# Residual beside the exponentials, sums beside the normalized weights, and a larger part of one output-weight unit kept on chip

## The chip, the core and the metric

The kernel runs on one core of a Trainium2 chip. The metric is the device time of one execution in microseconds. The core has a matrix engine (TensorE, in the profile PE for matmuls and PEld for weight loads), VectorE (DVE), ScalarE (ACT), GpSimd (POOL) and a queue that only issues DMAs (SyncE, SP). ScalarE and GpSimd can issue DMAs too. Each engine works through its own list of instructions in order and waits on semaphores for the others. On-chip memory has 128 partitions; matmul results go to PSUM banks.

## The reference

Two branches share one layer norm of x (2048 rows of 1024) and are added to x.

```python
xn = _layernorm(x, axis=-1)
return x + _A_ref(xn, A_mem0, A_Wq, A_Wk, A_Wv, A_Wo, A_seg_len) + _B_ref(xn, B_w1, B_b1, B_w2, B_b2)
```

Branch B is a dense layer to 3584, an approximate GELU and a dense layer back. Branch A is a recurrence over 64 segments of 32 rows:

```python
h = jnp.concatenate([mem, xs], axis=1)          # 8 memory rows, 32 rows of x
q, k, v = (einsum('btd,dhe->bhte', h, W) for W in (Wq, Wk, Wv))     # 32 heads of 128
p = _softmax(where(mask, einsum(q, k) * scale, -1e9))
o = einsum('bhte,hed->btd', einsum(p, v), Wo)
mem = o[:, :M, :]                               # handed to the next segment
outs.append(o[:, M:, :])
```

So each segment must have the memory rows of the one before, and each needs all four weights, 32 MB in bfloat16[...].

## The kernel before

**Two stages.** The first (up to L639) computes layer norm and branch B for all rows, and leaves in DRAM, for each segment, a row block `hr_d[s]` of 128 partitions by 512 columns. Its columns 0 to 255 are the turned x rows of segment s; columns 256 to 511 of block s + 1 hold the residual, x plus branch B, that is to be added to the output of segment s. The second stage is the loop over 64 segments (L715).

**A main row set and a left one.** A segment's main product takes 24 of its x rows and the 8 memory rows, 32 in all. The other 8 x rows of four segments are gathered to a left set of 32 rows, and pass through the weights once per group of four, spread over its segments. In segments with number 1 modulo 4 and in the last (`left_o`), one output product of 64 rows covers both sets. Such a segment has two residuals: `st["res"]` and, from `hrL_d`, `st["resL"]`.

**Weights.** The weights are cut into 64 units of 128 by 2048 (512 KB). The order of a segment is K, Q, K, Q, V, V in half passes of eight units and O of sixteen. 46 units stay in on-chip memory; 18 are streamed for each segment. Of these two are copied from PSUM banks (`IN_PSUM`, `IN_BANKS`), by VectorE at L246. One more (`PART`, the thirteenth of O counted from zero) is partly resident: its first `PART_COLS` = 768 columns stay in `part_home`, the others are loaded. The stream has six places; when TensorE has used a unit (`unit_done`), SyncE starts the load of the next into its place (`start_stream`), and waits for its turn in order.

**Small homes.** Three tensors at fixed places share a scratch area. `half_home` (1024 columns) is `part_home` in columns 0 to 767 and `pr_all`, the home of the exponentials of the attention scores, in the others. `hr_home` (512 columns) holds the x rows in columns 0 to 255, read by the K, Q and V products as `hT`, and `res_home` in columns 256 to 511. `pd_main` (320 columns) holds the normalized attention weights of the main keys, made by VectorE at L896 from the exponentials; L900 makes those of the left keys (`pd_left`) and is the last to read `pr_all`. The values product (L915) reads `pd_main`.

**Order around the change.** In half pass V, 1, after unit 4, `sums(1)` starts the second normalization: a product with ones on TensorE, a logarithm and two exponentials on ScalarE (L886, L889), then L896 and L900 on VectorE. At the end of that half pass, `load_x_rows(s + 1)` (L268) loads the next segment's block: for s + 1 above 5 all 512 columns in one DMA of 128 KB, x rows and residual together; before that 256 columns, and the residual by a DMA of its own at L1039. ScalarE issues these for segments 0 to 4, GpSimd for the others. The left residual is loaded into `pr_all` after O unit 1 (L1072). The values product of the second half stands after O unit 5 (in segments 3 modulo 4 after units 4 and 6). After O, the output goes to `o_sb` (L1081 or L1084), `put_mem` turns the eight memory rows on TensorE (L291) and writes them beside the x rows in `hr_home` (L295); the next segment's K pass reads both. Then the residual is added in place (L1104), and the sums are stored by GpSimd: four DMAs of 24 rows (L1137), or in `left_o` segments four to `outL_d` (L1109) and from there to the output (L1134).


Of the kernel before, what the change touches and what calls it, by code (L numbers as in the profile page):

```python
# [14 lines left out]
ALU = mybir.AluOpType  # L15
PSUM = bass.MemoryType.PSUM

P = 128
S = 2048
DM = 1024  # L20
# [17 lines left out]
NX = 24  # L38
# [16 lines left out]
WARM = 16  # L55
NPAIR = 9
AT_BANKS, AT_PART = 5, 4
PART_COLS = 768


def pass_order():
# [28 lines left out]
def kernel(  # L90
# [16 lines left out]
    nc = tc.nc  # L107
# [3 lines left out]
    out_flat = out.rearrange("b s d -> (b s) d")  # L111
# [6 lines left out]
    Wo_v = A_Wo.rearrange("h e d -> e h d")  # L118
# [6 lines left out]
    hr_d = dram.tile([NSEG + 1, P, 512], BF16, name="hr_d")  # L125
    hrL_d = dram.tile([NGRP + 1, P, 512], BF16, name="hrL_d")
# [13 lines left out]
    half_home = nc.alloc_sbuf_tensor_at("half_home", [P, DM], BF16, offset=SCRATCH)  # L140
    hr_home = nc.alloc_sbuf_tensor_at("hr_home", [P, 512], BF16, offset=SCRATCH + 2048)
    pd_main = nc.alloc_sbuf_tensor_at("pd_main", [P, 320], BF16, offset=SCRATCH + 3072)

    part_home, pr_all, res_home = half_home[:, 0:PART_COLS], half_home[:, PART_COLS:DM], hr_home[:, 256:512]
    slabs = ctx.enter_context(tc.tile_pool(name="slabs", bufs=1))
    consts = ctx.enter_context(tc.tile_pool(name="consts", bufs=1))
    hrp = ctx.enter_context(tc.tile_pool(name="hrp", bufs=1))
# [11 lines left out]

    qL_last = consts.tile([P, 16, SEG], BF16, name="qL_last")  # L160
    qL = [consts.tile([P, 16, SEG], BF16, name="qL"), qL_last]
    ident = res_home[:, 0:P]
    make_identity(nc, ident)
    ident_mem = consts.tile([P, 4, NL], BF16, name="ident_mem")
    nc.vector.tensor_copy(out=ident_mem[:, :, :], in_=ident.rearrange("p (j t) -> p j t", j=4)[:, :, NX:SEG])
# [2 lines left out]
    for j in range(4):  # L168
# [11 lines left out]
        out=m, in_=m, pattern=[[1, NX]], compare_op=ALU.is_ge, fill=0.0, base=0, channel_multiplier=-1,  # L180
    )
    for half in range(2):
        m = mask_left[0:SEG, :, 8 - 8 * half:16 - 8 * half]
        nc.gpsimd.affine_select(
            out=m, in_=m, pattern=[[-8, GRP], [0, 8]], compare_op=ALU.is_ge, fill=0.0, base=0, channel_multiplier=1,
        )
        nc.gpsimd.affine_select(
            out=m, in_=m, pattern=[[8, GRP], [1 if half else 0, 8]], compare_op=ALU.is_ge, fill=0.0,
# [28 lines left out]
    def fetch(t, unit):  # L217
        w, i, u = unit
        if unit == PART:
            h = 4 * i + 2 * u  # L220
            nc.sync.dma_start(out=t[:, 0:DM - PART_COLS], in_=Wo_v[:, h, PART_COLS:])
            nc.sync.dma_start(out=t[:, DM - PART_COLS:], in_=Wo_v[:, h + 1, :])
        elif w == "O":
            h = 4 * i + 2 * u
            nc.sync.dma_start(out=t.rearrange("p (h d) -> p h d", d=DM), in_=Wo_v[:, h:h + 2, :])
        else:
            nc.sync.dma_start(out=t, in_=W_v[w][:, i, 2048 * u:2048 * u + 2048])
# [36 lines left out]
    nxt, kept_in = {}, {}  # L264

    def load_x_rows(s, eng=nc.sync):
        n = 512 if s > 5 else 256
        eng.dma_start(out=hr_home[:, 0:n], in_=hr_d[s, :, 0:n])  # L268
        nxt["hT"] = hr_home[:, 0:256].rearrange("p (k t) -> p k t", k=KT)

    def load_left_rows(g, eng=nc.sync):
# [30 lines left out]
    with tc.tile_pool(name="ma", bufs=2) as ma, tc.tile_pool(name="mps", bufs=6, space=PSUM) as mps:  # L302
# [31 lines left out]
        for j in range(4):  # L334
            nc.sync.dma_start(
                out=o_sb[32 * j + NX:32 * j + 32, 0:8, :],
                in_=mem0[:, 256 * j:256 * j + 256].rearrange("m (h e) -> m h e", h=8),
# [4 lines left out]
        for i in range(14):  # L342
            t = slab(f"w2_{i}")[:, :].rearrange("p (c d) -> p c d", d=DM)
# [171 lines left out]
        for tg in range(4):  # L515
            last = tg == 3
            if last:
# [3 lines left out]
                h = 4 * IN_BANKS[1] + 2 * IN_BANKS[2]  # L521
# [12 lines left out]
            for fb in range(FC):  # L534
# [3 lines left out]
                else:  # L538
# [4 lines left out]
                    out=xb[:, :], in_=ps[:, :], func=ACT.Identity, bias=b1col[:, fb:fb + 1], scale=1.0  # L543
# [4 lines left out]
                    out=u[:, :], in0=u[:, :], scalar1=0.044715, scalar2=1.0, op0=ALU.mult, op1=ALU.add  # L548
# [96 lines left out]
    with tc.tile_pool(name="late", bufs=1) as late, \  # L645
# [69 lines left out]
        for s in range(NSEG):  # L715
# [15 lines left out]
            st = {}  # L731
# [301 lines left out]
            else:  # L1033
                at[1] = [lambda: values(0, (0, 1))]

            def load_res():
                st["res"] = res_home
                if s < 5:
                    nc.scalar.dma_start(out=res_home, in_=hr_d[s + 1, :, 256:512])  # L1039

            psV1, psV1L = half_pass("V", 1, left_v[1], at)
            st["V", 1] = values_out(psV1, sp.tile([P, 512], BF16, name="v", tag="a"), nc.scalar.copy)
# [1 line left out]
                left_values(1, psV1L)  # L1044
            if not final:
                load_x_rows(s + 1, nc.scalar if s < 5 else nc.gpsimd)
            else:
                nc.gpsimd.dma_start(out=res_home, in_=hr_d[s + 1, :, 256:512])
            if first:
                load_left_rows(g + 1, nc.gpsimd)  # L1050

# [4 lines left out]
                at = {5: [lambda: values(1, (0, 1))]}  # L1056
            if left_v[1] and not first:
                at[9] = [lambda: left_values(1, psV1L)]
            at.setdefault(0, []).append(load_res)
            psX = new_acc()  # L1060
            for n, unit in enumerate(O_UNITS):
                t = unit_tile(unit)
                if n == NPAIR and not left_o:
                    st["folded"] = fold(psX)
                    psX = new_acc()
                o_product(n, t, psX)
                unit_done(unit)
                for fn in at.get(n, ()):
                    fn()
                if n == 1 and left_o:  # L1070
                    st["resL"] = pr_all
                    (nc.scalar if s < 5 else nc.gpsimd).dma_start(  # L1072
                        out=st["resL"][:, :], in_=hrL_d[og, :, 256:512]
                    )
            nw = 2 if left_o else 1
            if not final:
                o_sb = nat_home
# [20 lines left out]
            for w, r in reversed(list(enumerate(tiles))):  # L1098
                if left_o:
                    o = psX[:, 256 * w:256 * w + 256].rearrange("p (h e) -> p h e", e=32)  # L1100
                else:
                    o = o_sb[:, 0:8, :]
                r_rows = r.rearrange("p (h e) -> p h e", e=32)
                nc.vector.tensor_tensor(out=r_rows, in0=o, in1=r_rows, op=ALU.add)  # L1104
                if left_o and not final:

                    for b in range(2):
                        c0 = 256 * (2 * b + w)
                        nc.gpsimd.dma_start(out=outL_d[og, :, c0:c0 + 256], in_=r[64 * b:64 * b + 64, :])  # L1109
# [5 lines left out]
            if final:  # L1115
                engines = [nc.sync, nc.scalar]
                n = 0
                for w, r in enumerate(tiles):
                    for b in range(2):
                        cs = slice(256 * (2 * b + w), 256 * (2 * b + w) + 256)  # L1120
                        pieces = [(rows, slice(64 * b + m0, 64 * b + m0 + NX))]
                        for sl, row in left_rows:
                            p0 = 64 * b + NL * sl
                            pieces.append((slice(row, row + NL), slice(p0, p0 + NL)))
                        for o, i in pieces:
                            engines[n % 2].dma_start(out=out_flat[o, cs], in_=r[i, :])
                            n += 1
            elif left_o:
                pairs = [(out_flat[rows, :], outL_d[og, m0:m0 + NX, :])]
                pairs += [  # L1130
                    (out_flat[row:row + NL, :], outL_d[og, NL * sl:NL * sl + NL, :]) for sl, row in left_rows
                ]
                for o, r in pairs:
                    small.append(lambda o=o, r=r: nc.gpsimd.dma_start(out=o, in_=r))  # L1134
            else:
                for j in range(4):
                    nc.gpsimd.dma_start(out=out_flat[rows, 256 * j:256 * j + 256], in_=res[32 * j:32 * j + NX, :])  # L1137
            if not final:
                hT = nxt["hT"]
        while small:  # L1140
# [34 lines left out]
```

## Time and profile before

| what | value |
|---|---|
| median of 3 runs (lowest, highest) | 1835.91 us (1828.53, 1837.86) |
| the profiled execution | 1839.26 us |
| its span (first to last instruction) | 1837.5 us |
| TensorE matmuls busy | 1717.9 us, 93% |
| VectorE, ScalarE, GpSimd busy | 955.3, 663.8, 284.4 us |
| bytes moved by DMA | 612.94 MB, mean 334 GB/s |
| start of the first segment's products | 417.4 us |
| loads of streamed O units | 256 of 512 KB, 64 of 320 KB |
| loads of x rows by GpSimd (L268) | 58 of 128 KB, 5.5 us to landing (median) |

The page gives each engine's busy time in 40 equal slices, a digit being tenths. A row of the list of waits reads: engine and instruction that stood idle, what ended the wait, the sum in us, how many times, the longest. A row of a timeline reads: start in us, length in us, engine, line, operation, what it writes and reads, and in brackets the idle time of the engine before it with what ended it. A GpSimd row of a DMA is the time to issue it, not to move the data.

### The profile page before, as it was taken

Reading aid. Unit: us, or ns where it says so; the run is one execution under the profiler, and the core shown is the slowest. Engines: PE = TensorE matmul, PEld = TensorE weight load, DVE = VectorE, ACT = ScalarE, POOL = GpSimd, SP = SyncE. Lnnn points to the kernel's source line nnn. Section 1 sums busy time; section 2 is a strip of 40 time slices with the busy share of each in tenths; the row PEclk is TensorE's granted clock in tenths of the full one; section 3 lists DMA queues with packets and bytes.
Section 4 is the critical chain, followed back from the end, with each engine's and each line's share of the span. In section 5 each row is a group of like instructions: output and inputs, shape, how many; then the busy total and the mean of one; then the engine's idle time right before and its main releaser. Section 6 shows DMA issues by size and latency. Waiting matters only on the chain.

```text
span 1837.5 us, 69927 instructions
## 1 busy us (share of the span) xinstructions
PE 1717.9 (93%) x30556; PEld 893.2 (49%) x30576; DVE 955.3 (52%) x2330; ACT 663.8 (36%) x1429; POOL 284.4 (15%) x559
## 2 busy tenths in 40 slices
PE   8999999998999999999999999999999999999997
PEld 4444444444454445454545545454545454545444
DVE  7657483805454545555454555455545454545543
ACT  6334251602333333333333333333333333333333
POOL 0000001501342111111111111112111111111111
PEclk9999999999999999999999999999999999999999
DMA  9931212769999999999999999999999999999998
GB/s 286 313 98 46 55 44 57 260 209 371 397 404 389 391 384 389 381 394 388 373 397 386 400 385 394 374 390 401 389 384 390 383 398 391 397 376 384 389 393 313
DMA packets 229278, 612.94 MB, mean 334 GB/s; under 512 B 46795, under 2 KB 76027, under 8 KB 228972
## 3 DMA queue, kind: packets, MB, share of 16 engines
q1 hardware_dynamic: 207252, 588.05, 84.3%
q0 software_dynamic: 17408, 17.69, 3.0%
q8 instruction: 239, 3.92, 0.8%
q10 hardware_dynamic: 4312, 2.73, 0.5%
q14 instruction: 67, 0.55, 0.1%
HBM read 594.40 MB, written 29.23 MB: 339 GB/s over the span
## 4 chain that ended last, share of the span: by engine, by line
PE 32%; DMA 18%; DVE 4%; ACT 2%; issue 1%; POOL 0%; DVEq 0%; ACTq 0%; SPq 0%
PE acc L739 22%; DMA u<-Wc_K 10%; PE acc L962 6%; DMA outL_d<-half_home 3%; DMA u<-Wc_O 3%; ACT mixed L889 1%; DVE b_oL L804 1%; PE acc L915 1%; DMA hr_home<-hr_d 1%; DVE pd_main L896 1%; PE mixed L848 1%; DMA u<-Wc_V 1%; ACT mixed L886 1%; DMA u<-Wc_Q 0%; PE mixed L854 0%
## 5 line engine op out<-in xcount | busy, mean ns | idle before, releaser
L739 PE MATMUL acc<-u,hr_home 128*32 128x512 bf16 x11520 | 770.8, 380 | 34.0 <-DMA u<-Wc_K 18.2
L739 PEld LDWEIGHTS <-hr_home 128*32 128x32 bf16 x12288 | 342.1, 96 | 317.3 <-issue 57.3
L739 PE MATMUL acc<-u,hrL 128*32 128x512 bf16 x2880 | 248.8, 379 | 3.0 <-DVE folded L978 3.0
L468 PE MATMUL ps<-u 128*128 128x512 bf16 (+1 forms) x920 | 195.7, 375 | 2.0 <-ACT u L388 2.0
L246 DVE TENSOR_SCALAR u<-kept 128x512 uint32<-128x512 uint32 x254 | 163.5, 685 | 35.4 <-PE acc L962 12.3
L962 PE MATMUL acc<-u,d_oL 128*32 128x512 bf16 (+1 forms) x1792 | 153.3, 381 | 11.7 <-DMA u<-Wc_O 9.4
L790 ACT CAST kT<-acc 128x512 bf16<-128x512 f32 x64 | 37.4, 585 | 307.6 <-PE acc L739 307.5
L589 PE MATMUL ps<-u 128*128 128x512 bf16 x657 | 146.2, 379 | 0.8
L962 PEld LDWEIGHTS <-b_oL 128*32 128x32 bf16 (+1 forms) x3381 | 108.4, 98 | 74.5 <-issue 35.9
L896 DVE TENSOR_TENSOR pd_main<-half_home,mixed 128x320 bf16<-128x320 bf16 x128 | 62.4, 487 | 153.2 <-ACT mixed L889 153.2
L468 PEld LDWEIGHTS <-u 128*128 128x128 bf16 x920 | 90.5, 99 | 105.5 <-issue 2.4
L1137 POOL DMA_DIRECT2D out_dram<-hr_home x188 | 96.3, 512 | 294.1 <-DVE hr_home L1104 280.5
L962 PE MATMUL acc<-u,b_oL 128*32 128x256 bf16 (+2 forms) x2062 | 117.1, 289 | 20.2 <-DMA u<-Wc_O 19.5
L804 DVE STREAM_TRANSPOSE b_oL<-b_oL 128x512 bf16<-128x512 bf16 x128 | 90.6, 708 | 64.8 <-ACT b_oL L790 64.8
L268 POOL DMA_DIRECT2D hr_home<-hr_d x58 | 32.8, 565 | 581.3 <-PE acc L739 576.1
L962 PEld LDWEIGHTS <-d_oL 128*32 128x32 bf16 (+1 forms) x2048 | 70.3, 99 | 84.7 <-issue 28.0
L739 PEld LDWEIGHTS <-hrL 128*32 128x32 bf16 x3072 | 82.9, 96 | 51.2 <-issue 7.7
L790 ACT CAST b_oL<-acc 128x512 bf16<-128x512 f32 x128 | 75.1, 587 | 86.1 <-PE acc L739 86.1
L589 PEld LDWEIGHTS <-u 128*128 128x128 bf16 x672 | 65.3, 98 | 77.3 <-DVE g_u L550 0.4
L889 ACT ACTIVATE mixed<-mixed,small_consts 128x160 f32<-128x160 f32 x256 | 94.2, 368 | 8.4
L542 ACT ACTIVATE g_xb<-ps,b1col 128x512 bf16<-128x512 f32 x112 | 76.8, 686 | 55.5 <-PE ps L468 54.7
L794 ACT CAST v<-acc 128x512 bf16<-128x512 f32 x128 | 75.1, 587 | 48.9 <-PE acc L739 48.6
(129 smaller groups left out, 2011.6 us busy)
## 6 DMA issues: line engine op xcount, KB each, us to landing
u<-Wc_K SPq DMA_DIRECT2D x320, 512.0 KB
u<-Wc_V SPq DMA_DIRECT2D x256, 512.0 KB
u<-Wc_O SPq DMA_DIRECT2D x256, 512.0 KB
u<-Wc_Q SPq DMA_DIRECT2D x128, 512.0 KB
u<-Wc_O SPq DMA_DIRECT2D x64, 320.0 KB
u<-in_B_w_dram SPq DMA_DIRECT2D x28, 512.0 KB
hr_home<-hr_d POOLq DMA_DIRECT2D x58, 128.0 KB, 5.5
u<-in_A_Wq_dram SPq DMA_DIRECT2D x14, 512.0 KB
```

What stands on the lines that cost most here:

```text
L246: nc.vector.tensor_single_scalar(out=out, in_=in_, scalar=0, op=ALU.bitwise_or)
L468: nc.tensor.matmul(ps[:, SEG * s0:SEG * s1].rearrange("p (s t) -> p s t", t=SEG), lhsT=w1_sb[fb // 2][:, kt, (fb % 2) * P:(fb % 2 + 1) * P ...
L542: nc.scalar.activation(out=xb[:, :], in_=ps[:, :], func=ACT.Identity, bias=b1col[:, fb:fb + 1], scale=1.0)
L589: nc.tensor.matmul(ps[:, :], lhsT=gts[fc // 4][:, fc % 4, t * P:(t + 1) * P], rhs=w2_sb[fc // 2][:, fc % 2, cs], start=(fc == 0), stop=(fc ...
L739: nc.tensor.matmul(o, lhsT=lhs[:, i, :], rhs=m, start=(i == seq[0]), stop=(i == seq[-1]), tile_position=(0, 32 * j),)
L790: cp(out=out, in_=ps.rearrange("p (h e) -> p h e", e=32))
L794: cp(out=t[:, :], in_=ps[:, :])
L804: nc.vector.transpose(out=home, in_=home)
L889: nc.scalar.activation(out=mixed[:, 160 * b:160 * b + 160], in_=mixed[:, 0:160], func=ACT.Exp, scale=-1.0, bias=off[:, b:b + 1],)
L896: nc.vector.tensor_tensor(out=pdA.rearrange("p c b q -> p b c q"), in0=prA[:, None, :, :].to_broadcast([P, 2, 4, 40]), in1=dd, op=ALU.mult,)
L962: nc.tensor.matmul(acc[r0:r0 + rows, c:c + wide], lhsT=lhs[:, 4 * (i % 4) + 2 * u + k, :], rhs=cols, start=start, stop=stop, tile_position ...
L1137: nc.gpsimd.dma_start(out=out_flat[rows, 256 * j:256 * j + 256], in_=res[32 * j:32 * j + NX, :])
```

## The change

`PART_COLS` goes from 768 to 1024, so `part_home` fills `half_home`, and the streamed rest of the unit is 1024 columns (256 KB). `pr_all` moves to the place in `hr_home` where `res_home` was, and the residual, which lived there, is loaded into `pr_all` once the exponentials are used up; with two residuals the left one goes there and the main one to `pd_main`. The sum of output and residual is written to `pd_main` in segments with one residual, and in place in those with two; the stores read from there.

`load_x_rows` now loads only the x rows. The residual has a DMA of its own in all segments, on the same engine as before: from segment 5 on it is issued after unit 6 of half pass V, 1, ahead of the x rows' load (in `left_o` segments the left residual there, and the main one after O unit 6); in segments 0 to 4 after O unit 0.

```diff
-PART_COLS = 768
+PART_COLS = 1024
...
-    part_home, pr_all, res_home = half_home[:, 0:PART_COLS], half_home[:, PART_COLS:DM], hr_home[:, 256:512]
+    part_home, pr_all = half_home[:, 0:PART_COLS], hr_home[:, 256:512]
...
-            nc.sync.dma_start(out=t[:, 0:DM - PART_COLS], in_=Wo_v[:, h, PART_COLS:])
-            nc.sync.dma_start(out=t[:, DM - PART_COLS:], in_=Wo_v[:, h + 1, :])
+            nc.sync.dma_start(out=t, in_=Wo_v[:, h + 1, :])
...
     def load_x_rows(s, eng=nc.sync):
-        n = 512 if s > 5 else 256
-        eng.dma_start(out=hr_home[:, 0:n], in_=hr_d[s, :, 0:n])
+        eng.dma_start(out=hr_home[:, 0:256], in_=hr_d[s, :, 0:256])
...
+            eng_res = nc.scalar if s < 5 else nc.gpsimd
+
             def load_res():
-                st["res"] = res_home
-                if s < 5:
-                    nc.scalar.dma_start(out=res_home, in_=hr_d[s + 1, :, 256:512])
+                st["res"] = pd_main[:, 0:256] if left_o else pr_all
+                eng_res.dma_start(out=st["res"], in_=hr_d[s + 1, :, 256:512])
+
+            def load_resL():
+                st["resL"] = pr_all
+                eng_res.dma_start(out=st["resL"], in_=hrL_d[og, :, 256:512])
+
+            if s >= 5:
+                at.setdefault(6, []).append(load_resL if left_o else load_res)
 
             psV1, psV1L = half_pass("V", 1, left_v[1], at)
...
                 load_x_rows(s + 1, nc.scalar if s < 5 else nc.gpsimd)
-            else:
-                nc.gpsimd.dma_start(out=res_home, in_=hr_d[s + 1, :, 256:512])
...
-            at.setdefault(0, []).append(load_res)
+            if left_o:
+                at.setdefault(6, []).append(load_res)
+            if s < 5:
+                at.setdefault(0, []).append(load_resL if left_o else load_res)
...
-                if n == 1 and left_o:
-                    st["resL"] = pr_all
-                    (nc.scalar if s < 5 else nc.gpsimd).dma_start(
-                        out=st["resL"][:, :], in_=hrL_d[og, :, 256:512]
-                    )
...
-                nc.vector.tensor_tensor(out=r_rows, in0=o, in1=r_rows, op=ALU.add)
+                sums_home = r if left_o else pd_main[:, 0:256]
+                nc.vector.tensor_tensor(
+                    out=sums_home.rearrange("p (h e) -> p h e", e=32), in0=o, in1=r_rows, op=ALU.add
+                )
...
-                    nc.gpsimd.dma_start(out=out_flat[rows, 256 * j:256 * j + 256], in_=res[32 * j:32 * j + NX, :])
+                    nc.gpsimd.dma_start(out=out_flat[rows, 256 * j:256 * j + 256], in_=pd_main[32 * j:32 * j + NX, 0:256])
```

More of the change, by code (lines that the diff above doesn't have):

```diff
@@ L161 @@
     qL = [consts.tile([P, 16, SEG], BF16, name="qL"), qL_last]
-    ident = res_home[:, 0:P]
+    ident = pr_all[:, 0:P]
     make_identity(nc, ident)
```

## The prediction

> **What bounds the kernel now.** I read the page's slices first, then the stages, the waits, and last the timeline of single segment boundaries. The page: from slice 10 on (the 64 segments) TensorE and the DMA engines are both full.
>
> ```profile
> PE   8999999998999999999999999999999999999997
> ...
> DMA  9931212769999999999999999999999999999998
> ```
>
> The stages (columns: length; busy us and count of each engine; clock; DMA share; GB/s) say which of the two it is. The DMA share is 1.01, its records overlapping a little; TensorE is busy 277 of 300 us, waits inside its pipeline included.
>
> ```profile
> 600.00:900.00 300.00, 278.03 (x6151) 150.07 (x6147) 155.01 (x373) 106.57 (x249) 45.40 (x87) 1.00 1.01 388
> 900.00:1200.00 300.00, 277.01 (x6039) 148.12 (x6032) 151.43 (x367) 106.05 (x247) 47.76 (x92) 0.99 1.01 387
> ```
>
> So weight streaming at 388 GB/s is the bound, but by how much? The waits give TensorE's margin (waited for: us in total, times, longest).
>
> ```profile
> POOL hr_home L268 <- PE acc L739: 576.1, 57, 14.3
> PE acc L962 <- DMA u<-Wc_O: 28.9, 62, 1.3
> PE acc L739 <- DMA u<-Wc_K: 18.2, 34, 1.9
> POOL half_home L1072 <- DVE pd_left L900: 15.0, 10, 6.6
> DVE hr_home L295 <- DMA hr_home<-hr_d: 11.1, 14, 3.2
> ```
>
> TensorE waits only some 47 us in 1,400 for weights: a second bound is close behind. The last line is the warning: the memory rows of the next segment (L295) must wait for the load of its x rows (L268), a load that GpSimd can issue only when V's last product has released hr_home (first line). One boundary on VectorE and GpSimd, in segment 40:
>
> ```profile
> 1321.74 0.56 POOL L268 DMA_DIRECT2D hr_home<-hr_d  x1 [12.07 <-PE acc L739]
> ```
>
> ```profile
> 1322.30 0.28 DVE L900 TENSOR_TENSOR pd_left<-half_home,mixed 128x128 bf16<-128x128 bf16 x1
> ...
> 1326.08 0.42 DVE L1084 TENSOR_TENSOR d_oL<-acc,folded 128x256 bf16<-128x256 f32 x1 [0.42 <-PE acc L962]
> 1327.41 0.22 DVE L295 CAST hr_home<-mixed 128x64 bf16<-128x64 f32 x1 [0.91 <-DMA hr_home<-hr_d]
> ```
>
> The load leaves at 1321.74 and lands 5.6 us later; VectorE idles 0.91 us for it, and the next segment's first product waits with it. Note that pd_left, the last reader of the exponentials, ends at 1322.58, after the x load has left.
>
> I walked this timeline through the 58 segments whose x load is GpSimd's. By the segment's number mod 4 (class 1 has the combined output product), after the O pass's first product: the x load is issued at +0.60, +0.48, +0.64, +0.42 us (classes 0 to 3); pd_left ends at +1.44, +1.17, +1.44, +0.79; the load lands 0.09, 2.34, 0.40, 0.89 us on average before L295 starts. In 24 of 58 it is the last to come.
>
> **What the skill says.** The Trainium skill, "DMA: Bandwidth & Descriptors", section "Issuing engines are not separate DMA queues": transfers of all engines share the same 16 DMA engines. The trace agrees, share 1.01, so fewer streamed bytes are worth time. Same page, "Anatomy of one DMA — SWDGE (gpsimd) path": a semaphore wait happens on the issuing sequencer before dispatch, not in the DMA engine, so a waiting issue holds what stands behind it. The trace agrees: L1072 stood 15.0 us on GpSimd for pd_left. The section also puts the fixed cost at about 2 us; here, beside the full stream, the x load takes 4.0 to 7.1 us (median 5.5), and the measurement decides.
>
> **The change, part by part.**
>
> 1. Stream. The partly resident unit streams 256 KB a segment instead of 320: 128 packets of 2,560 bytes (median 102 ns in the trace's packet records) become 2,048 (84 ns in the early stages). 64 x 128 x 18 ns / 16 = 9.2 us less DMA time; by bytes, 4.19 MB at 388 GB/s, 10.8 us. I take 10.
>
> 2. Matmuls. The combined product loses one split pair in each of 17 segments: 17 x some 0.05 us = 1 us, nothing.
>
> 3. Residual, segments 5 on, classes 0, 2, 3. It no longer rides in the x load (128 KB); a 64 KB load of its own goes into the exponentials' home. It stands on GpSimd's queue ahead of the x load and must wait for pd_left. L1072, which waits for the same instruction today, starts 0.75 us after pd_left's end. An issue takes 0.56, the next follows 0.03 later. So the x load leaves at pd_left + 1.34: +2.78, +2.51, +2.78, +2.13 us after the first O product, later by 2.18, 2.03, 2.14, 1.71. Less the present margins, boundary by boundary: L295 is late by 2.09, 0.10, 1.74, 0.81 us, 4.7 per four segments. Queued behind the waiting load on GpSimd is just the x load; behind that L295, and with it the next segment's K pass.
>
> 4. Class 1: the left residual (64 KB) moves ahead of the x load likewise, covered by 2.34 us; the main residual goes to pd_main after the values product, lands about when L1104 needs it, at worst half a us late on VectorE, where only weight copies (L246) stand behind.
>
> 5. Sums go to pd_main, whose next writer is L896 of the next segment. Today the stores at these places land 1.6 to 2.7 us ahead of that L896 on average over a class (0.8 at the least): covered, and a later boundary moves both. The sum itself is one DVE instruction as before. The x load no longer shares hr_home's waits on stores, which had long ended anyway.
>
> 6. Segments 0 to 4: ScalarE issues x before residual as before; residual waits there for pd_left, about 1 us, with no ScalarE work due until the values copy. Nothing.
>
> 7. 58 more DMA completions and smaller rows: 58 x 16 marks of 9 ns over 16 engines = 0.5 us. An x load of half the size is one packet per engine, not two; between nothing (the 64 KB L1072 load takes 5.0 against 5.5 median, but at lower backlog no less) and 0.5 us per boundary. I take 0.3, or 0.8 per four segments.
>
> **The sum.** TensorE's path grows by 4.7 - 0.8 = 3.9 us per four segments. What takes it up: weight waits in the K, Q and V passes, behind L295. Counted as start-to-start excess over 213 ns of four products released by a weight DMA, they are 2.5, 19.1, 0.7, 7.1 us in classes 0 to 3, 1.8 per four segments. The O pass's waits (39.7 us by the same count) lie beside the x load and don't help directly. That leaves 2.1. Then the stream gets ahead, its backlog shrinks, and the x load lands sooner: over 54 loads, landing time rises 0.41 us per us of backlog. A backlog 1.2 us shorter (its lowest tenth lies only 1.8 us above its minimum, so not much more is to be had) gives 0.41 x 1.2 x 2.7 boundaries = 1.3. So +0.8 us per four segments, x 14.5 = 12 us. The 10 us of DMA time saved is then slack. The profiled execution took 1839.3 us; 1851 on its scale. The median shown is 3.4 lower: 1848.
>
> **Rivals.**
>
> *DMA stays the bound*: the six-place ring takes up all the lateness, and the bytes saved are time, 10 us: 1826. For it: share 1.01, 39.7 us of O waits. Against it: x lateness of 3.9 exceeds the 1.8 that lies in series with it. It decides if the x load lands some 0.8 us sooner than I think (2.1 over 2.7 boundaries), after 4.4 us instead of 5.2.
>
> *Nothing gives*: lateness 4.7 less 1.8, times 14.5: +42, 1878. For it: landing time depends weakly on backlog (4.4 us even at the lowest). Against it: in the early stage at about 200 GB/s GpSimd's loads land in some 3 us, so relief comes once the stream pauses.
>
> *A wash*: relief of 2 us per four segments and a few us of bytes saved: within 9 us of before.
>
> *Stores late*: L896 waits for the sums' stores. Margin 1.6 us; each us beyond it costs up to 1 us per segment on the attention chain. It needs a residual that lands over 1.6 us after L295; as it is issued 0.56 us ahead of the x load, which L295 itself needs, it doesn't.
>
> **Chances.** 0.5% (9 us, from 1826.7 to 1845.1) is about what can be told from no change. Forecast (+6 to +25): 0.45; nothing gives or stores late: 0.15; wash: 0.20; DMA stays the bound: 0.20, near the border itself. Slower 0.53, same 0.27, faster 0.20. Range 1824 to 1874; the likeliest case alone 1842 to 1861.
>
> **What would show it.** Right: waits of L295 for the x load's DMA grow from 11 us and 14 times to over 50 us in some 40 boundaries; x load issued about 1.34 us after pd_left; GpSimd's wait shifts from the V product to pd_left; weight waits in K fall below 10 us; DMA share below 1, near 0.98. Wrong: K and O waits for weights as before with share 1.01 (DMA bound), or an x load that leaves before pd_left's end.

## The result and the profile after

| | before | after |
|---|---|---|
| median of 6 runs (lowest, highest), us | 1836.88 (1828.53, 1843.54) | 1988.95 (1978.0, 2007.33) |
| span of the profiled execution, us | 1837.5 | 1976.2 |
| bytes moved by DMA, MB | 612.94 | 608.76 |

The changed kernel takes 1.0844 times as long [1.0781, 1.0907]: slower by 152 us, where 12 was forecast and 1874 was the range's upper end. The direction was right, the size too small by a factor of more than twelve.

I read the views in the same order as before. First the page's slices of the kernel after (rows: busy tenths in 40 equal slices).

```profile
PE   9999999998888888888888888888888888889887
...
DMA  9921215689899999999999999999999999999997
```

From slice 10 on TensorE fell from nines to eights and the DMA engines still show nines, which says only "90% or more". The stages are finer (columns: length; busy us and count of PE, PEld, DVE, ACT, POOL; clock; DMA share; GB/s).

```profile
600.00:900.00 300.00, 262.15 (x5684) 136.40 (x5680) 139.09 (x341) 100.63 (x235) 48.24 (x92) 0.98 0.96 355
900.00:1200.00 300.00, 261.12 (x5512) 135.16 (x5508) 138.69 (x336) 95.25 (x222) 49.59 (x95) 0.96 0.95 349
```

The DMA share fell from 1.01 to 0.95 and the stream from 387 to 350 GB/s, TensorE from 277 to 262 us busy of 300. Both of the old bounds now wait for something else. The clock is a little lower too (0.98 and 0.96, was 1.00 and 0.99); O passes, which TensorE fills, did not become longer for it: over the four classes of segments they last 5.5, 7.6, 6.0 and 5.1 us, before 5.2, 7.7, 6.2 and 5.0, 24 us together in both. The list of waits names what they wait for (us in total, times, longest).

```profile
DVE hr_home L293 <- DMA hr_home<-hr_d: 111.6, 44, 4.0
PEld L737 <- DVE hr_home L293: 108.8, 63, 4.1
...
DVE pd_main L1107 <- DMA pd_main<-hr_d: 62.1, 16, 5.2
...
PEld L737 <- DVE pd_main L1107: 47.8, 14, 4.4
...
PE acc L737 <- DMA u<-Wc_K: 0.7, 2, 0.4
```

Two waits carry the loss. The memory rows (L293, formerly L295) wait for the x load in 44 boundaries instead of 14, 111.6 us instead of 11.1, and the first K product stands behind them. The other is new: in combined segments (class 1, and the last, with one O product for both row sets) the sum (L1107) waits up to 5.2 us for the main residual's load into `pd_main`, and TensorE's K and Q products wait for that sum. TensorE's waits for streamed K units, 18.2 us before, are gone. The chain that ended last says the same in shares of the span: the loads from `hr_d` hold 17% of it.

```profile
PE acc L737 20%; DMA hr_home<-hr_d 13%; PE ps L466 10%; PE ps L587 7%; DMA pd_main<-hr_d 4%; PE acc L960 3%; DMA u<-Wc_O 2%; PE ps L620 2%; PE acc L913 1%; POOL hr_home L1038 1%; ACT mixed L887 1%; DVE u L245 1%; DMA u<-Wc_K 1%; DVE b_oL L802 1%; PE pT L620 1%
```

**One ordinary boundary.** The timeline of the kernel after at the end of segment 36 (class 0), GpSimd first, then VectorE (start, length, engine, line, what it does, idle time before it and its releaser).

```profile
1310.48 0.56 POOL L1038 DMA_DIRECT2D hr_home<-hr_d  x1 [13.39 <-PE acc L919]
1311.20 0.55 POOL L266 DMA_DIRECT2D hr_home<-hr_d  x1 [0.16 <-issue]
```

```profile
1309.45 0.28 DVE L898 TENSOR_TENSOR pd_left<-hr_home,mixed 128x128 bf16<-128x128 bf16 x1
...
1313.91 0.42 DVE L1086 TENSOR_TENSOR d_oL<-acc,folded 128x256 bf16<-128x256 f32 x1 [0.46 <-PE acc L960]
1317.84 0.22 DVE L293 CAST hr_home<-mixed 128x64 bf16<-128x64 f32 x1 [3.50 <-DMA hr_home<-hr_d]
```

This is step 3 of the prediction at work. pd_left ends at 1309.73, the waiting residual load leaves 0.75 us later, the x load 0.72 after that, and VectorE stands 3.50 us for its landing.

**One combined boundary.** The same views at the end of segment 37 (class 1), GpSimd, then VectorE, then TensorE.

```profile
1335.13 0.56 POOL L1042 DMA_DIRECT2D hr_home<-hrL_d  x1 [14.40 <-PE acc L960]
1336.14 0.57 POOL L266 DMA_DIRECT2D hr_home<-hr_d  x1 [0.45 <-PE acc L960]
1340.88 0.54 POOL L1038 DMA_DIRECT2D pd_main<-hr_d  x1 [4.17 <-PE acc L960]
```

```profile
1347.17 0.42 DVE L1107 TENSOR_TENSOR pd_main<-acc,pd_main 128x256 bf16<-128x256 f32 x1 [4.93 <-DMA pd_main<-hr_d]
```

```profile
1347.65 1.59 PE L737 MATMUL acc<-u,hr_home 128*32 128x512 bf16 x20 [3.66 <-DVE pd_main L1107]
```

The sum reads the O product out of a PSUM bank (`acc`). The second half pass of the next segment, Q, needs that bank, so TensorE stops 3.66 us in the middle of its products. Why does the main residual leave only at 1340.88? The only thing that its issue waits for by the code is the values product, the last reader of `pd_main`, which ended at 1336.2. The releaser that the view names, an O product, is a guess from the nearest event. What fits is another time: the left residual (L1042), the older of the two GpSimd loads then in flight, landed 0.33 us before this issue. So it is in all of the 14 combined segments with number above 5 short of the last, 0.33 us each time, whether the younger load (the x load) was still in flight (13 of them) or not.

Averaged over the segments of a class (number mod 4, from segment 6 on; "period" from one writing of the memory rows to the next; the other columns count from the O pass's first product, but for the landing time, which counts from the x load's issue):

```
class   period        boundary to O    x load leaves   it lands after   memory rows written
        before after  before after     before after    before after     before after
0       20.83  23.44  14.65  14.16     0.60   2.93     5.40   6.26      6.19   9.28
1       23.79  23.05  15.09  14.45     0.46   2.65     5.73   5.27      8.70   8.60
2       20.99  26.03  13.88  17.18     0.65   2.82     6.01   5.88      7.11   8.85
3       22.02  24.03  15.45  15.86     0.44   2.19     5.22   5.86      6.58   8.18
```

Four segments take 96.55 instead of 87.63 us. Times 14.3 groups that is 128 us; the first five boundaries lost 8.7 more; together 137 of the 139 us between the spans. Of the 8.9 us, 6.3 come from memory rows that are written later (+3.09, -0.10, +1.74, +1.60) and 2.6 from the K to V passes, of which class 2, the segment after a combined one, alone lost 3.3. Most of the early loss is in segment 3, 29.8 instead of 22.9 us. VectorE's timeline of the kernel after shows why:

```profile
511.86 0.49 DVE L894 TENSOR_TENSOR pd_main<-hr_home,mixed 128x320 bf16<-128x320 bf16 x1 [7.34 <-DMA out_dram<-pd_main]
```

The weights of the next segment cannot be written to `pd_main` before the sums stored from there have left; there the stores stand on GpSimd behind small DMAs of branch B.

### The profile page after: what moved, and what is told of

Read it like the earlier page. It is cut to its first block, busy times and chain, and to the rows that moved or that the text cites. A ratio compares the mean times of both kernels' runs of the same rounds, so it can differ in the third digit from the quotient of the medians.

```text
span 1976.2 us, 70105 instructions
## 1 busy us (share of the span) xinstructions
PE 1753.4 (89%) x30559; PEld 888.4 (45%) x30559; DVE 951.4 (48%) x2330; ACT 662.5 (34%) x1429; POOL 316.2 (16%) x617
## 2 busy tenths in 40 slices
DMA packets 229952, 608.76 MB, mean 308 GB/s; under 512 B 47707, under 2 KB 76683, under 8 KB 229628
## 4 chain that ended last, share of the span: by engine, by line
PE 45%; issue 25%; DMA 22%; DVE 4%; POOL 2%; ACT 2%; POOLq 0%; DVEq 0%; ACTq 0%; SPq 0%
PE acc L737 20%; DMA hr_home<-hr_d 13%; PE ps L466 10%; PE ps L587 7%; DMA pd_main<-hr_d 4%; PE acc L960 3%; DMA u<-Wc_O 2%; PE ps L620 2%; PE acc L913 1%; POOL hr_home L1038 1%; ACT mixed L887 1%; DVE u L245 1%; DMA u<-Wc_K 1%; DVE b_oL L802 1%; PE pT L620 1%
## 5 line engine op out<-in xcount | busy, mean ns | idle before, releaser
L737 PE MATMUL acc<-u,hr_home 128*32 128x512 bf16 x11520 | 796.3, 392 | 137.7 <-DVE hr_home L293 84.1
L737 PE MATMUL acc<-u,hrL 128*32 128x512 bf16 x2880 | 252.9, 384 | 4.2 <-DVE folded L976 2.9
L1142 POOL DMA_DIRECT2D out_dram<-pd_main x188 | 95.9, 515 | 295.2 <-DVE pd_main L1107 287.9
L894 DVE TENSOR_TENSOR pd_main<-hr_home,mixed 128x320 bf16<-128x320 bf16 x128 | 62.4, 487 | 161.7 <-ACT mixed L887 150.7
L960 PE MATMUL acc<-u,b_oL 128*32 128x256 bf16 (+1 forms) x1998 | 113.1, 292 | 21.5 <-DMA u<-Wc_O 21.3
L1038 POOL DMA_DIRECT2D hr_home<-hr_d x43 | 24.2, 564 | 501.7 <-PE acc L919 226.1
L293 DVE CAST hr_home<-mixed 128x64 bf16<-128x64 f32 x63 | 14.1, 224 | 160.9 <-DMA hr_home<-hr_d 111.6
```

The source lines that it names most:

```text
L737: nc.tensor.matmul(o, lhsT=lhs[:, i, :], rhs=m, start=(i == seq[0]), stop=(i == seq[-1]), tile_position=(0, 32 * j),)
L894: nc.vector.tensor_tensor(out=pdA.rearrange("p c b q -> p b c q"), in0=prA[:, None, :, :].to_broadcast([P, 2, 4, 40]), in1=dd, op=ALU.mult,)
L960: nc.tensor.matmul(acc[r0:r0 + rows, c:c + wide], lhsT=lhs[:, 4 * (i % 4) + 2 * u + k, :], rhs=cols, start=start, stop=stop, tile_position ...
```

## The experiments

**The theories.** Theory A: the loss is the two late loads, the x load behind a residual that waits for pd_left, and the main residual of combined segments. Its rivals put the loss on the DMA system instead: on more and smaller loads beside the full stream, or on how the bytes are moved. Where the text on record names further rivals by letter, it says what they hold. All edits are against the kernel after, unless another is named; every ratio is to the kernel before on the same chip, with its 95% interval.

**E1: the residual behind the x load.** From segment 5 on the residual is issued where segments 0 to 4 have it, after O unit 0.

```diff
-            if s >= 5:
-                at.setdefault(6, []).append(load_resL if left_o else load_res)
...
-            if s < 5:
-                at.setdefault(0, []).append(load_resL if left_o else load_res)
+            at.setdefault(0, []).append(load_resL if left_o else load_res)
```

> Edit: from segment 5 on the residual (in combined segments the left one) is issued after O unit 0, behind the x load instead of ahead of it. Theory A (the x load is held behind a load that waits for pd_left): the time from the first O product to the write of the memory rows falls back from 9.3, 8.9, 8.2 us (classes 0, 2, 3) to about 6.2, 7.1, 6.6, some 90 us in all; what stays is the 3.3 us per four segments behind combined segments: 1890 to 1910 us. Rival B (the loads are slow because they are now two of 512-byte rows and share a home with the exponentials, whatever their order): 1970 to 1990 us.

Measured: 1869.59 us, 1.0146 [1.0091, 1.02], by the medians 119 us less than after. The waits:

```profile
DVE pd_main L1103 <- DMA pd_main<-hr_d: 27.8, 16, 2.9
PEld L737 <- DVE hr_home L293: 19.4, 63, 1.6
PEld L737 <- DVE pd_main L1103: 13.4, 13, 2.1
...
DVE hr_home L293 <- DMA hr_home<-hr_d: 3.2, 4, 1.0
```

The memory rows no longer wait for the x load (3.2 us), and the DMA share is 1.00. The gain exceeds what theory A expected of this edit because it helps the other wait as well: the older load in flight is now the x load, which leaves sooner, and the third load still starts 0.33 us after its landing, in all of those segments. The sum (L1103 here) waits 27.8 us instead of 62.1.

**E2: the main residual of combined segments by ScalarE.** Order otherwise as in the kernel after.

```diff
-                eng_res.dma_start(out=st["res"], in_=hr_d[s + 1, :, 256:512])
+                (nc.scalar if left_o else eng_res).dma_start(out=st["res"], in_=hr_d[s + 1, :, 256:512])
```

> Edit: only the main residual of combined segments (into pd_main after O unit 6) is issued by ScalarE instead of GpSimd. Theory A (GpSimd starts a third load only 0.33 us after the oldest of two in flight has landed, so this one leaves at the end of O, and the sum, the PSUM bank and the next Q pass wait for it): the load leaves some 4 us sooner, the products stop waiting for L1107 (41 us now), and the K to V passes of class 2 fall from 17.2 to about 14 us: 1935 to 1950 us. Rival C (the load is late because pd_main is released late by the values product): the load leaves when it does now and the time stays at 1980 to 1995.

Measured: 1930.95 us, 1.0456 [1.0385, 1.0527]. The load now leaves 3.52 us after the O pass's first product, with the values product; after had 6.3 to 8.0. TensorE's list of waits has 0.2 us for the sum, and all of the x load's wait:

```profile
PE acc L737 <- DVE hr_home L293: 89.8, 43, 4.1
PE acc L737 <- DVE pd_main L1107: 0.2, 1, 0.2
```

Class 2 fell from 26.0 to 22.6 us. So the late third load was worth 58 us by the medians, 71 by the ratios, and it was not the values product that held it: only the engine that issued it changed.

**E3: without the bytes.** The partly resident unit is cut as before, all else as after.

```diff
-PART_COLS = 1024
+PART_COLS = 768
```

> Edit: 768 columns of the partly resident unit kept as in the kernel before; homes, loads and order as in the changed kernel. Theory A (streaming is no longer the bound; DMA share is 0.95): within 5 us of the changed kernel, 1984 to 1995. Rival D (bytes still set the pace in part): 10 us slower than the changed kernel or more, 2000.

Measured: 1980.28 us, 1.0748 [1.0682, 1.0815]. Not slower than after: the 64 KB per segment that the change keeps on chip are worth nothing while other waits hold the kernel up.

**E4: both repairs**, E1 and E2 together.

> Edit: both of the edits above: residual behind the x load, and the main residual of combined segments issued by ScalarE. Theory A: both losses gone, streaming is the bound again with 64 KB less a segment: 1826 to 1850 us, and the DMA share back at 1.0. Rival B (small loads, shared home): 1900 or more.

Measured: 1856.98 us, 1.0073 [1.0046, 1.01]. Most of the loss is gone, yet the gain expected from the saved bytes does not appear, though the stream is full again:

```profile
600.00:900.00 300.00, 276.56 (x6073) 146.86 (x6069) 151.05 (x366) 108.18 (x253) 49.95 (x95) 1.00 1.00 381
900.00:1200.00 300.00, 279.51 (x6087) 148.50 (x6076) 153.06 (x370) 106.05 (x247) 53.36 (x102) 1.00 1.01 387
```

What remains in the profile is 22 us of span: 10.1 us until the memory rows of segment 5 (segment 3 takes 31.3), and 0.9 us per four segments behind them. The last segment lost nothing: its sums start 0.04 us after the O pass ends, as before. The 4 us that the expectation of E7 (below) puts there are a wait of VectorE for the O product.

**E5: the bytes alone.** From the kernel before, 64 KB less are streamed per segment; columns 768 to 1023 of the unit are not loaded, and 512 to 767 are used twice in their place, so that part of the O product is another.

```diff
-            nc.sync.dma_start(out=t[:, PART_COLS:], in_=copies[unit])
+            nc.sync.dma_start(out=t[:, DM:], in_=copies[unit][:, DM - PART_COLS:])
...
+                if unit == PART and k == 0:
+                    return [
+                        (256 * n, 256, part_home[:, 256 * min(b, 2):256 * min(b, 2) + 256]) for n, b in enumerate(blocks)
+                    ]
+                homes = [t for b in blocks]
```

> Edit, on the kernel before: the streamed part of the partly resident unit is 1024 columns instead of 1280, nothing else moves; columns 768 to 1023 of the unit are not loaded and its columns 512 to 767 are used twice, so this kernel leaves that quarter of one weight row block out. What 64 KB less a segment are worth alone, with streaming the bound: 10 us faster than the kernel before (ratio 0.994 to 0.996). If TensorE's own path is as close a bound as its 47 us of weight waits suggest, less: 0 to 5 us.

Measured: 1848.72 us, 1.0026 [1.0002, 1.005]: no gain, against an expected 0.4 to 0.6%. The DMA share stays at 1.00 to 1.01, and TensorE's waits for units only shrink:

```profile
PE acc L966 <- DMA u<-Wc_O: 22.6, 54, 1.2
PE acc L739 <- DMA u<-Wc_K: 14.2, 28, 1.6
```

Before they were 28.9 and 18.2. In one profile of each kernel, some 10 us less waiting in the two rows go with no shorter run. So a share of 1.01 did not mean that bytes are time. That TensorE's own chain is an equally close bound, and takes up what the stream gives, fits with this but was not shown by taking work off TensorE.

**E6: a larger descriptor area for GpSimd.** The kernel sets `SCRATCH` = 384 bytes per partition aside for the descriptors of GpSimd's DMAs, in before and in after. With `PART_COLS` at 768 the exponentials go back to `half_home`, and the 512 bytes gained enlarge that area. The residuals' homes and waits are those of after, so E3 is its partner.

```diff
-SCRATCH = 384
-SMALL = 3712
+SCRATCH = 896
+SMALL = 3200
...
-    part_home, pr_all = half_home[:, 0:PART_COLS], hr_home[:, 256:512]
+    part_home, pr_all = half_home[:, 0:PART_COLS], half_home[:, PART_COLS:DM]
```

> Edit, on the changed kernel with 768 columns kept (1980 us): the exponentials' home back in half_home, and the 512 bytes per partition that this frees given to GpSimd's DMA descriptor area (896 instead of 384 bytes per partition); order and homes of the residuals as in the changed kernel. Theory A (GpSimd's descriptor area holds two loads of 128 rows, so a third waits for the oldest to land): the main residual of combined segments leaves about 3.6 us after the first O product instead of 6.3 to 8, TensorE no longer waits for L1107, about 50 us less: 1925 to 1945. Rival C (something else of the values product holds it): 1970 to 1990.

Measured: 1901.55 us, 1.0314 [1.0268, 1.0361], against 1.0748 for E3: some 80 us by the ratios, where theory A had about 50. The third load no longer waits for the first to land. GpSimd's timeline of E6 at a combined boundary:

```profile
1298.72 0.56 POOL L1043 DMA_DIRECT2D half_home<-hrL_d  x1 [14.15 <-PE acc L961]
1299.71 0.55 POOL L267 DMA_DIRECT2D hr_home<-hr_d  x1 [0.43 <-PE acc L961]
1300.42 0.54 POOL L1039 DMA_DIRECT2D pd_main<-hr_d  x1 [0.16 <-issue]
```

0.71 us lie between the last two issues; in segment 37 of after it was 4.74. In each of the 14 segments the third leaves 2.3 to 4.3 us before the first has landed. With 384 bytes two loads of 128 rows fit, and a third is held by the area, whatever it waits for by its program. The wait for the x load is still there, as theory A has it (memory rows 105.9 us in 46 boundaries). Segment 3 shrinks too, from 31.7 us in E3 to 22.3: the four stores that it waits for now leave in one row, while in after the third stood 2.80 us and left 0.30 us after an older DMA had landed. This is some 9 of the 80 us.

**E7: every residual by ScalarE**, after O unit 0 (main of combined segments after unit 6, of the last into the free home of x), and the stores of segments 0 to 4 by ScalarE.

```diff
-            eng_res = nc.scalar if s < 5 else nc.gpsimd
+            eng_res = nc.scalar
...
-            if s >= 5:
-                at.setdefault(6, []).append(load_resL if left_o else load_res)
...
-                    nc.gpsimd.dma_start(out=out_flat[rows, 256 * j:256 * j + 256], in_=pd_main[32 * j:32 * j + NX, 0:256])
+                    (nc.scalar if s < 5 else nc.gpsimd).dma_start(out=out_flat[rows, 256 * j:256 * j + 256], in_=pd_main[32 * j:32 * j + NX, 0:256])
```

> Edit, on the changed kernel: all residual loads issued by ScalarE after O unit 0 (main one of combined segments after unit 6), so that GpSimd's x load stands behind nothing; in segments 0 to 4 the four stores of sums issued by ScalarE (they stood behind small DMAs on GpSimd, 7 us in segment 3); in the last segment the main residual goes to the x rows' home at O unit 0 (4 us). Theory A: the 13 us by which the version with both edits trails the kernel before are these places, and the bytes saved show: ratio 0.993 to 1.000. If saved bytes are worth nothing here: 0.999 to 1.003.

Measured: 1846.98 us, 1.0001 [0.9982, 1.0021]. With nothing of the residual and no early store on GpSimd the change costs nothing, and gains nothing: the whole loss lay in where and when those DMAs are issued. Up to the memory rows of segment 5 the profile is within 1.5 us of before's.

**E8: a load ahead of the x load that need not wait.** `PART_COLS` at 768 leaves a quarter of `half_home` free. The main residual goes there in all segments, issued by GpSimd ahead of the x load; the left one is issued by ScalarE after O unit 0.

```diff
-                st["res"] = pd_main[:, 0:256] if left_o else pr_all
+                st["res"] = half_home[:, PART_COLS:DM]
...
-                eng_res.dma_start(out=st["resL"], in_=hrL_d[og, :, 256:512])
+                nc.scalar.dma_start(out=st["resL"], in_=hrL_d[og, :, 256:512])
```

> Edit, on the changed kernel with 768 columns kept: the main residual, still a load of its own and still ahead of the x load on GpSimd, goes to the free 256 columns of half_home, which nothing holds, instead of the exponentials' home or pd_main; the left residual is issued by ScalarE after O unit 0. Theory A (not the split into two loads and not the order, but the wait for pd_left in front of the x load): the x load leaves 0.5 us after the first O product as before, and the time is within 10 us of the kernel before (ratio 1.000 to 1.006; segment 3's stores may cost 7 us). Rival B (two loads of 512-byte rows cost it): ratio 1.03 or more.

Measured: 1850.55 us, 1.0041 [1.0024, 1.0057], some of it segment 3 (26.8 us). A separate load in front, with its issue and its packets, costs next to nothing. Not every x load left as early as before, though: in classes 0, 1 and 3 it did (+0.68, +0.51, +0.40 us), in class 2 it left at +1.53, in most boundaries 0.34 us after a small store of GpSimd had landed. The memory rows of class 2 were written only 0.1 us later for it (7.21 us, before 7.11).

**E9: the wait without the second load.** One 128 KB load as before, but its residual half lands in the exponentials' home, so all of it must wait for pd_left (`PART_COLS` 768; the left residual goes to the free quarter).

```diff
-        eng.dma_start(out=hr_home[:, 0:256], in_=hr_d[s, :, 0:256])
+        n = 512 if s > 5 else 256
+        eng.dma_start(out=hr_home[:, 0:n], in_=hr_d[s, :, 0:n])
...
-                st["res"] = pd_main[:, 0:256] if left_o else pr_all
-                eng_res.dma_start(out=st["res"], in_=hr_d[s + 1, :, 256:512])
+                st["res"] = pr_all
+                if s < 5 or final:
+                    eng_res.dma_start(out=st["res"], in_=hr_d[s + 1, :, 256:512])
```

> Edit, on the changed kernel with 768 columns kept: x rows and residual in one 128 KB load after half pass V, 1 as in the kernel before, into a home that now holds the exponentials, so that this one load waits for pd_left; the left residual goes to the free 256 columns of half_home. It takes the price of the wait alone, with no second load ahead. The x load leaves 0.75 us after pd_left (+2.2, +1.5 us after the first O product) instead of +2.9, +2.2 in the changed kernel and +0.6, +0.4 in the kernel before. If the time is the wait's: the memory rows are late by 1.6 to 2 us per boundary in classes 0, 2, 3 less 1.8 us per four segments, some 40 to 60 us: ratio 1.02 to 1.035. If the second load ahead of it made the larger part: ratio below 1.015.

Measured: 1910.04 us, 1.0348 [1.0296, 1.0399]. Its waits:

```profile
DVE hr_home L295 <- DMA hr_home<-hr_d: 98.2, 45, 4.2
...
ACT hr_home L860 <- DMA outL_d<-hr_home: 29.1, 16, 2.8
```

E8 and E9 part the two things that step 3 had joined: the load in front is harmless, the wait is not. Of the 64 us some 7 are segment 3 (30.0 us) and a part is the second line, exponentials that wait for a store from their home, of which the kernel after has 2.5 us. So the wait alone is worth at most 57 us; E6, with wait and load and neither of those, lost 58. The load left at +1.6 to +2.2 us, earlier than after's (+2.2 to +2.9), and took 6.76, 5.53, 5.98, 5.76 us to land: against before's, of the same size, 1.4 us longer in class 0 and 0.5 in class 3, but no longer in classes 1 and 2.

**E10: the x load by ScalarE too**, ahead of its copy of V, on top of E7.

```diff
+            if not final:
+                load_x_rows(s + 1, nc.scalar)
             st["V", 1] = values_out(psV1, sp.tile([P, 512], BF16, name="v", tag="a"), nc.scalar.copy)
...
-            if not final:
-                load_x_rows(s + 1, nc.scalar if s < 5 else nc.gpsimd)
```

> Edit, on the version with all residual loads on ScalarE (ratio 1.000): the x load too is issued by ScalarE, ahead of V's copy, so that GpSimd's issue time and queue are out of the path to the memory rows. If the x load lands sooner (an issue of 0.33 instead of 0.56 us) the memory rows come sooner where it is last, and the saved bytes can show: ratio 0.985 to 0.998. If ScalarE's loads wait behind the weight stream: 1.00 to 1.02.

Measured: 1845.18 us, 1.001 [0.9993, 1.0027]. Issuing the x load from another queue gives nothing more here.

**E11: sums in place**, on top of E7: the sums stay in the exponentials' home and are stored from there.

```diff
-                sums_home = r if left_o else pd_main[:, 0:256]
+                sums_home = r
...
+                    (nc.scalar if s < 5 else nc.gpsimd).dma_start(out=out_flat[rows, 256 * j:256 * j + 256], in_=res[32 * j:32 * j + NX, :])
```

> Edit, on the version with all residual loads on ScalarE (ratio 1.000): the sums of segments with one residual are written in place, over the residual in the exponentials' home, and stored from there, instead of to pd_main. The next segment's first exponential must then wait for the stores: these land about 7.8 us after the memory rows are written, the exponential starts at 6.7 to 7.1. If that wait is on the path: about 1 us in three of four segments, ratio 1.01 to 1.03. If TensorE has other work meanwhile: 0.998 to 1.005.

Measured: 1902.41 us, 1.0317 [1.0281, 1.0353], 3.2% above E7's ratio. ScalarE's exponentials (L858) of the next segment wait for the stores to leave their home:

```profile
ACT hr_home L858 <- DMA u<-Wc_V: 54.2, 36, 2.7
...
ACT hr_home L858 <- DMA out_dram<-hr_home: 28.2, 18, 3.1
```

The first of these rows names a weight load, which an exponential does not read; a store that ended near it is the likelier releaser. So storing from `pd_main`, which is written later in the segment, is what makes the shared home bearable: worth 58 us here. Sums moved (E7) and bytes saved (E5) are both neutral against before.

No version is faster than the kernel before beyond its interval.

## Why the prediction was wrong

**Step 1, the stream, 10 us:** wrong. E5 has the bytes alone at 1.0026 [1.0002, 1.005], and E3 has them worth nothing in the slow kernel. "The trace agrees, share 1.01, so fewer streamed bytes are worth time" was the error: TensorE waited just 47 us for weights, and E5 shows that those waits can shrink without a gain. The sum itself had put these 10 us down as slack, so the error did not make the miss; it carried the rival "DMA stays the bound".

**Step 3, the residual ahead of the x load:** the mechanism was right, and the issue times were too. The x load left later by 2.33, 2.19, 2.17, 1.75 us in classes 0 to 3, against a forecast 2.18, 2.03, 2.14, 1.71. The lateness of the memory rows was forecast as 4.7 us per four segments and came to 6.3, mostly through class 0 (3.09 for 2.09) and class 3 (1.60 for 0.81). The difference lies in the landing, below. Before the change the list of waits has 14 boundaries in which L295 waited for this load, where the prediction counts 24.

**Step 4, the main residual of combined segments:** failed, and this is one of the two large errors. "Lands about when L1104 needs it, at worst half a us late on VectorE, where only weight copies (L246) stand behind." First, the load does not leave with the values product, at +3.5 us, but at +6.3 to +8.0, since a third GpSimd load is held until the oldest has landed (E6, E2). Secondly, behind the sum stands more than a weight copy: its PSUM bank, and so the next segment's Q products. The kernel before has at most two such loads at a boundary, but its trace shows the same hold among the small DMAs of the early segments. GpSimd's timeline of the kernel before in segment 2:

```profile
490.12 0.54 POOL L457 DMA_DIRECT2D hrL_d<-R_n  x1 [1.18 <-issue]
```

This DMA waits for no semaphore, and yet stood 1.18 us; it left 0.33 us after an older one of 128 rows (issued at 484.42) had landed. Counted by E2 step 4 cost 58 to 71 us.

**Steps 5 and 6, sums to pd_main and segments 0 to 4:** the margin held from segment 6 on (L894 waited for stores twice in the whole run, 7.3 us in segment 3 and 2.2 in segment 5). "Nothing" for segments 0 to 4 was wrong by about 7 us, in segment 3, where the stores stand behind other GpSimd DMAs and are held as above. The rival "Stores late" was right in these early segments alone. E11 shows that the move of the sums, priced at nothing, saves 58 us that the shared home of the residual would cost.

**Step 7, the smaller load 0.3 us sooner:** did not come, since a landing time was taken to be the same whenever the load leaves. Landing times changed by +0.86, -0.46, -0.13 and +0.64 us. For a load that leaves when before's did the size was not far off: in E7 it lands in 5.06, 5.55, 5.44 and 4.87 us, 0.2 to 0.6 sooner than before's. Part of that belongs to the lighter stream, for the 128 KB load of E5 lands 0.15 to 0.27 us sooner as well.

**The sum, the relief:** failed, the other large error. I took 1.3 us per four segments for x loads that land sooner once the stream gets ahead, from a slope of 0.41 us per us of backlog. The DMA share did fall to 0.95, and landing times did not. The share is an average: from the packet records of segments 6 to 61, it was 0.99 while the x loads were under way (1.00 before), and 0.93 from their landing to the next O pass (1.01 before). So the stream thinned where TensorE waited, not where the x load needed it. That slope described how loads differed within a full stream; nothing showed that it would hold as a lever when the stream slows elsewhere. The absorption of 1.8 us by weight waits was real in size (the waits for K units fell from 18.2 to 0.7 us, 1.2 per four segments; K to V passes of classes 0 and 1 are 1.1 us shorter together), but classes 2 and 3 lost 3.7 there.

So of the forecast's 0.8 us per four segments: lateness 6.3 instead of 4.7 less 0.8 for smaller loads; absorption about 1.1 instead of 1.8, relief 0 instead of 1.3; and 3.7 in the K to V passes that the sum did not have. That makes 8.9. The rival "Nothing gives" (+42) had the waiting part nearly right: E6, which has that part alone, is 58 us slower than before. What no rival had is the third load.

As for the signs set out ahead: the wait of L295 grew to 111.6 us in 44 boundaries (over 50 us and some 40 forecast), K's weight waits fell below 10, and the share below 1. GpSimd's wait did shift from the V product to pd_left by its times; in the list of waits it stands under the O and values products, which end close by.

## What to carry to other kernels

When a load is moved ahead of another on an in-order queue, ask separately what it must wait for and how many loads that queue can have in flight: here a load in front cost nothing, its wait some 58 us, and a third load in flight as much again. Follow a late instruction to everything that it holds, the PSUM bank that it reads among it, not only to what stands behind it on its engine. And do not take a slope seen among transfers in a full stream as a relief that will come when the stream slows: ask in which part of a segment it will slow. Nor take a DMA share of 1.01 as a price for bytes.

## What was not expected of the hardware

- GpSimd's DMAs are limited by their descriptor area. With 384 bytes per partition two loads of 128 rows were in flight, and the third left 0.33 us after the oldest had landed, in all 14 combined segments from 9 to 61 of after, E1 and E3; with 896 bytes it left 2.3 to 4.3 us ahead of that landing (E6). The timeline put this hold down to an unrelated O product, or to "issue".
- At a DMA share of 1.00 to 1.01 in both, 64 KB less per segment (4 MB in all) gave 1.0026 [1.0002, 1.005].
- In class 0 an x load issued later in the O pass took longer to land, with the DMA engines about as busy meanwhile: 5.40 us when issued at +0.60 (before, 128 KB, share during the flights 0.98) and 5.06 at +0.59 (E7, 64 KB, 0.99), but 6.26 at +2.93 (after, 64 KB, 0.98) and 6.76 at +2.18 (E9, 128 KB). In class 1 it took no longer. What delays it was not found.
